# Two interleaved attention layers: the second follows five steps behind the first instead of eight, and the feed-forward runs on 64+64 tokens every two steps

## The chip, the cores and the metric

The kernel runs on one core of one Trainium2 chip. The metric is device microseconds of one execution; the figure of the kernel before is the median of three runs. A profile of one execution, taken by the hardware profiler, stands beside it. Engines are named as in the profile: PE (TensorE matmul), PEld (its weight loads), DVE (VectorE), ACT (ScalarE), POOL (GpSimd), SP (SyncE, which issues most DMAs).

## What is computed

The reference takes 2048 tokens of width 576 and applies attention, feed-forward, attention, feed-forward, each with a layer norm before it and a residual sum after it. Both attention layers use the same weights, both feed-forwards too. Cut to what matters:

```python
def _A_ref(x, mem0, Wq, Wk, Wv, Wo, seg_len):     # 32 heads of 128, 8 memory rows, segments of 32
    mem = mem0
    for s in range(n_seg):                         # 64 segments, one after the other
        xs = x[:, s * seg_len:(s + 1) * seg_len, :]
        h = jnp.concatenate([mem, xs], axis=1)     # 40 rows
        q, k, v = h @ Wq, h @ Wk, h @ Wv           # per head
        p = softmax(where(mask, q @ k.T * scale, -1e9))
        o = (p @ v) @ Wo
        mem = o[:, :M, :]                          # the next segment needs this
        outs.append(o[:, M:, :])
def _B_ref(x, w1, w3, w2):                         # 576 -> 4608 -> 576
    return (silu(x @ w1) * (x @ w3)) @ w2
x = x + _A_ref(_layernorm(x), ...); x = x + _B_ref(_layernorm(x), ...)
x = x + _A_ref(_layernorm(x), ...); x = x + _B_ref(_layernorm(x), ...)
```

The memory rows tie each segment to the one before it, so a layer's 64 segments are a chain.

## The kernel before, in words

**Steps.** The work goes in steps. Step t computes segment t of layer one and segment t − LAG of layer two together, as one operand of 80 columns (twice 32 tokens and 8 memory rows). With LAG = 8 there are 72 steps: 0 to 7 hold layer one alone, 8 to 63 both layers, 64 to 71 layer two alone. A one-layer step has operands of 40 columns.

**A step on PE** consists of batches, each with a letter (`KINDS`): eight Q (queries and keys of four heads, 32 matmuls) with eight q (their last 64 of the 576 rows, as two row tiles side by side), four S (scores of a group of eight heads), four T (transposed probabilities), four P (values), four O (output projection, 32 matmuls) with four o (its last 64 columns, as column tiles). Values: in two-layer steps they are computed for a pair of steps, four G with tails g (`vg`, 128 rows by 512 columns) and one narrow V with tail v (`vm`, memory rows of the even step); one-layer steps use X and V. The results of a G go to the tile V in two halves of 64 rows (`vg_out`), the second after the P of its group.

**Feed-forward.** A job (`job`, L454) takes 128 tokens of each layer, every four steps: p (transposes of the attention output, `post_tr`), two layer norms with transposes n into XTB, then 18 units of 256 hidden columns: F (`ffn_up`, 16 matmuls of 256 columns) with tail f, tanh on ACT, two products on DVE, and for each two units and each layer a W or w (`ffn_down`, 8 matmuls of 288 columns) that DVE adds to the residual XR. There are 18 jobs: the first two and the last two hold one layer only (128 columns). Each job but the last streams all feed-forward weights from HBM through SP: per unit w1, w3 (`load_w13`, four DMAs into one of two W13 slots) and w2 (`load_w2`, one of two W2C slots); a slot is loaded again when the F or W that read it is done. The last job's weights replace the attention weights in the tiles W and WV (`tail_load`). After its job a layer-one group gets a layer norm of its own (L1tr, letter b) and is written into HT, the transposed input of the attention; layer one's own inputs (L0tr, letter a) are loaded through SP and normed in groups of 128.

**Order.** The order of PE is a string of letters, `FIRST + FOUR * 11 + LAST` (16 steps, 11 times four steps, 12 steps and the final job). `plan` (L76) places the work of the other engines, queue by queue, around it by list scheduling with a cost for each node (`actc`, `dve`, `EW_LAT`, `dma_bw`) and slots of limited pools (`POOLS`: PSUM banks, W13, HTT and so on); each engine then runs its instructions in that order and waits on semaphores where it must. PE batches have a tiling mode (full, column, row, or smaller tiles); batches that may run in either full or column mode take the mode of their neighbours, and in column mode `mm` (L586) issues each matmul as two of 64 columns of weights.

**Helpers.** All PE instructions stand at L591, ACT at L594, DVE at L597, SP's DMAs at L600; in the profile they are told apart by tiles. POOL clears the tile PB (L1010) and takes the power in the layer norm (L760).

Of the kernel before, what the change touches and what calls it, by code (L numbers as in the profile page):

```python
# [7 lines left out]
BF = mybir.dt.bfloat16  # L8
# [15 lines left out]
NPR = FF // (2 * P)  # L24
# [4 lines left out]
LAG = 8  # L29
R_HT = 6  # L30
# [3 lines left out]
EW_LAT = 0.135  # L34
NOW = 1.0e18
POOLS = {"bank": 8, "qkt": 4, "sme": 2, "pb": 2, "pts": 1, "ot": 4,
         "xr": 3, "xn": 2, "w13": 2, "w2": 2, "htt": 4}


def role(t):  # L40

    return (t - LAG) % 2
# [9 lines left out]
class Node:  # L52
# [11 lines left out]
    def after(self, *more):  # L64
        for d in more:
# [6 lines left out]
KINDS = {"m0tr": "m", "L0tr": "a", "L1tr": "b", "POST": "p", "Ftr": "n", "QK": "Q", "QKt": "q", "SC": "S", "TR": "T", "PV": "P",  # L72
         "WO": "O", "WOt": "o", "VX": "X", "VXt": "x", "VM": "V", "VMt": "v", "FF": "F", "FFt": "f", "VG": "G", "VGt": "g", "W2": "W", "W2b": "w"}


def plan(nodes, pools, letters):  # L76
# [42 lines left out]
    while len(order) < len(nodes):  # L119
# [46 lines left out]
        for m in n.outs:  # L166
            m.ready = max(m.ready, n.end + (0.0 if m.eng == e == "PE" else n.lat))
            m.left -= 1
            if m.left == 0:
                push(m)  # L170
# [5 lines left out]
def actc(*ns):  # L176

    return sum(max(0.067 + n * 0.000833, 0.19) for n in ns)


def dve(*ns):
    return sum(max(0.065 + n / 960.0, 0.19) for n in ns)


def dveh(*ns):

    return sum(max(0.065 + n / 1920.0, 0.19) for n in ns)
# [6 lines left out]
def ewh(*ns):  # L194
# [3 lines left out]

FIRST = (
    "amQQQQqqqqSSqqQQQTSQqqSxXVvPTPTOPOOTooPoOoQQqqqqQSQvqqSVQQqTqSQPQOSToPXTOPTxoPOOooQqqqQQSVvqQQSQqqqQSqTQPOSTPTOP"  # L200
    "OToooPaOoQQqqqqQQSvSVQqqqQQQSqTPSXTOPTOPoTxoPOOooQQpQqqqvVqSnQQSFfqFQqfqqQTQSPFTfSOFPWOToPFToffPOOooWQqqqqQQSQQS"
    "FFfqfVvqTQWQqSFxffqQFPSXTWfPFTOPOTOPFOooooWQfqqqQQSFqfqVvQQSFfqTQPWQSqqfFTQOSfoPFTOPWFTOPooffOoFQqqQqqvSQQWSVqqf"
    "FQQWqqSTQPQSTOPabOTXPooTOPxxOooXqqpQQQqqSQnVvfSFTQqqqQQPSFffqQFTOPoSWTFfPOOTFPWOooofQQqfqqFSQFqqfgQGWTQPQSfqFQQq"
    "fqFSWTGFSggfGPGTOPOTfgFaPOOooooWVvqqfQQFFQSqfqQWQSqqfFQTQQqfqSFPWTSFPOTfoOPFWTOPffFOoooWQQqqqqQSbQQQqgqSGSTGPQTq"
    "gqQPOggSGTGPOTOPoooOoQqqqpQVpSQnQvqqqQnQFSTffqFQQPqSwTFPSffOOWTFPFTOPWOoooowFffqqQQQWSfqqFQwQSFqfqgGTQQPWfqSTFFg"
    "gfqGQwPGTOoSPFgfOGTOPWOoooFqqfqQQQQvSwqVSFqqfQQWwTFPQfqfqFTQSwPWSfFOTFPWwOTffFPOOaooooWQQqqqqQwSbQGQgqqSQTQPQqqg"
    "SGTSGPGggTOPOTOPoooOo"
)
FOUR = (
    "QvqqpQQpQqqVSSnnQQFqfqfFQTQfqqWSFPwTFPSfOOTFPwTOPWOooooFffqqQQQQqqSWFSFffqgGQTQPQQgqqqGSwTFPGSfgfgFTGOPOWTOPwOoo"  # L210
    "ooFqqQQQQqfqVvSSwWFfqfqQQTFWQwQSFffqqFPWTOPSowTFPffOTOFPWwOoooFqqfqQQQWQSqqqaQSQQbQqgqSGTSGPgTGPOTggOPGTOPwOoooo"
)
LAST = (
    "QqqqpQQQSnpQQqqqVSvTSnQFffqPFOQqTwPoSWTFPffFTOOWPwOoooFFqfqQQQqqfSQQwQfqqFTSGSqfgQFPWQgfqGTSFPGFTfggOOPGTOPwWOoo"
    "ooFFqffqQQwQWQSqqVSvqqQQTFQPSfqqQwTOWSPFTFPofOTOPwOoooWFfqfqQQQQqfqSFwWvVSFTfqqQQPWQqqSvTQVSPOTbOPwOTooPoxOoXqQp"
    "pVvQqqqQSQQnqqSQnqQFTSfqQPFTSOPfTFOPwTOPWOooooFqfqfQQQSVqqqvQQQwSfqFWTFPSfqqQTQOPSFTwfFPOTOPWOooooFfqqQQQSqfxvVX"
    "qfFQwWTSQFQqqqfQPWSTwFPffqQFTWSOwFPffOFTOPwOooooWFvqfqQQQSWqqVQwSFfqqfQFTQQSqqWPQTPSOoTOPwOToobPxOoXqqqQQQpvSVqQ"
    "qQSnqQFfSTQFPqqfQOTSFfPwTOoofPFTOPFOfoowQqqQFSQfqqqQQSVvqqfQFTQFSfqPQOTowPSFTfxXPOTOPFOooowVvqqQQQSqqfQQSqqfQFST"
    "QQPwqqFTSOfPFTOfPwTOPfoooOoFQQqqqqQSQQSqqQVvSfTFPqQQwqfTSFPOTOFPTOPfoooOoFpwnfffFFwFwfffFFFwfffFFwFwfffFFFwfffFF"
    "wFwfffFFFfww"  # L220
)
ORDER = FIRST + FOUR * 11 + LAST


class Opt:

    qk, qkt, sc, tr, pv, wo, wog, vm = 0.0079, -0.0342, 0.0268, 0.1447, 0.0406, 0.2653, 0.0725, 0.1407
    vmt, vx, vxt, ff, fft, win, w2, gstep = -0.0231, 0.2313, 0.0843, 0.2124, -0.1839, 0.8 * (LAG - 4), 0.1943, 0.0624
    ustep, mode_pen, hor, wait, bulk, ff_split, last_win, tail_at = 0.0315, 0.1194, 0.0162, 0.141, 0.02, False, 2.5, -1.5


def make_nodes(em, nseg, pools, o=Opt, dma_bw=230e3, load_bw=400e3):

    ngrp = nseg // 4
# [10 lines left out]
    nst = nseg + LAG  # L245
    kb = lambda rows, cols: rows * cols * 2

    def layers_of(t):
        return [li for li in (0, 1) if 0 <= t - LAG * li < nseg]

    def both(t):

        return len(layers_of(t - role(t))) == 2

# [5 lines left out]
    ld_t = [load("ldt", kb(3 * R64, 4096), -10.0, em.load_tails(0)), node("ACT", 0.1, em.load_tails(1), prio=-120, name="ldt", lat=6.0)]  # L260
    node("ACT", 0.1, em.load_tails(2), prio=-80, name="ldt", lat=6.0)
    ld_h = [load("ldqk", kb(512, 4096), half - 9.0, em.load_qk(half)) for half in (0, 1)]
# [4 lines left out]
    m0t = node("PE", 0.3, em.m0_tr(b[0]), deps=[ld_m0], prio=-5, mode="full", acq=b, name="m0tr")  # L267
    m0e = node("DVE", 0.5, em.m0_ev(b[0]), deps=[m0t], prio=-5, rel=b, name="m0ev")

    xr = {}  # L270
    ht_ready = {}
    reads_ht = {}
    yx = {}
    ht_mem = {t: [] for t in range(nst + 1)}
    steps = [{} for _ in range(nst)]

    def ln_nodes(tag, src, xn, deps, prio, writes, warm=False):

        a = node("DVE", 1.16, em.ln_stats(src, xn), deps=deps, prio=prio, acq=[] if src is xn else [xn], name=tag + "stats")
        p_ = node("POOL", 0.45, em.ln_pow(xn), deps=[a], prio=prio, name=tag + "pow")  # L280
        c = node("DVE", 0.46 if src is xn else 0.66, em.ln_norm(src, xn), deps=[p_], prio=prio, name=tag + "norm")
        b = Slot("bank", users=len(writes))
        d = node("PE", 5 * 0.056, em.ln_tr(xn, b, warm), deps=[c], prio=prio, mode="full/col", acq=[b], rel=[xn], name=tag + "tr")
        out = []
        for wr, cost, more in writes:
            out.append(node("AD", cost, wr(b), deps=[d] + more + out[-1:], prio=prio, rel=[b], name=tag + "wr"))
        return out

    def ht_writes(li, g):

        out, at = [], {}
        for j in range(4):
            at.setdefault((4 * g + j - role(4 * g + j + LAG * li)), []).append(j)
        for te, js in at.items():
            te += LAG * li - R_HT
            cost = ewh(240, 80, 80) if li and both(te + R_HT) else ewh(160 * len(js))
            out.append(((lambda js: lambda b: em.ht_write(li, g, js, b))(js), cost, reads_ht.get(te, []) + reads_ht.get(te + 1, [])))
        return out

    def ht_set(li, g, nodes_):  # L300
        i = -1
        for j in range(4):
            t = 4 * g + j + LAG * li
            i += j == 0 or role(t) == 0
            ht_ready[li, t] = nodes_[i]


    vx_ev, last_v, pvs = {}, [], {}

    def v_nodes(name, t, k, prio, tail_at, emit, strips, deps, tail_deps, free):  # L310

        modes = ("col", "quad") if strips[0][3] == R64 else ("c32", "oct")
        b = banks()
        m_ = node("PE", 8 * 0.2158, emit(b, False), deps=deps, prio=prio, mode=modes[0], acq=b, name=name)
        n = node("PE", 0.2158, emit(b, True), deps=deps + tail_deps, prio=prio + tail_at, mode=modes[1], acq=b, name=name + "t")
        reads_ht.setdefault(t, []).extend([m_, n])
        for r in (0, 1):
            outs = em.v_parts(strips, r)
            b[r].users = len(outs)
            for p0, width, row, blk in outs:  # L320
                e = node("AD", (0.55, 0.6), em.v_ev(b[r], p0, width, row, blk), deps=[m_, n] + free.get(blk // 2, []), prio=prio + 0.01 * (blk // 2),
                         rel=[b[r]], name=name + "e")
                vx_ev.setdefault((name, t, blk // 2), []).append(e)
        return [m_, n]

    def paired(t):

        return role(t) == 1 and both(t) and t + 1 < nst and both(t + 1)

    def vg_nodes(t, g, deps, tail_deps):  # L330

        b = banks()
        for s in b:
            s.users = 2
        m_ = node("PE", 8 * 0.2158, em.vg(t, g, b, False), deps=deps, prio=t + o.vm, mode="full/col", acq=b, name="VG")
        n = node("PE", 0.2158, em.vg(t, g, b, True), deps=deps + tail_deps, prio=t + o.vm, mode="row", acq=b, name="VGt")
        for s in (t, t + 1):
            reads_ht.setdefault(s, []).extend([m_, n])
        return b, [m_, n]

    def vg_out(t, g, b, deps, row):

        return [node("AD", (0.55, 0.6), em.v_ev(b[r], row, R64, row, 2 * g + r), deps=deps, prio=t + o.vm + 0.01 * g + (0.05 if row == 0 else 0.0), rel=[b[r]],
                     name="VGe") for r in (0, 1)]

    def vx_pair(t, prio):

        if t and paired(t - 1):
            return
# [982 lines left out]
```

## Time and profile before

| | us |
|---|---|
| median of three runs (2683.0 to 2690.0) | 2684.11 |
| profiled execution, first to last instruction | 2684.2 |
| PE busy | 2621.2 (98%) |
| DVE busy | 2111.8 (79%) |
| ACT busy | 1346.4 (50%) |
| POOL busy | 332.2 (12%) |
| DMA engines, mean share | SP's queue 38.7%, 120 GB/s in all |
| TensorE clock granted | 0.995 of full |

The span of the profiled execution equals the median of the runs to 0.1 us, so sums made against the profile hold for the runs too. Engine times are sums of what each engine is busy; a busy PE is the union of pipelined matmuls, whose ends are modelled, so the cost of a batch is read from the start of its first matmul to the start of the next batch. In the timeline a row is "start us, duration us, engine, line, operation, tiles, shape, count"; successive instructions of one kind are merged into one row, and a row's duration holds some 0.16 us of pipeline that overlaps the next row. A step's end is read from the copy into the tile YO (ACT), one for each step: the first, of step 0, starts at 58.3 us, that of step 3 at 125.1, of step 7 at 238.2, of step 63 at 2403.6, of step 71 at 2641.6.

### The profile page before, as it was taken

What the parts mean: (1) busy time and instruction counts of PE and PEld (TensorE: products, weight loads), DVE (VectorE), ACT (ScalarE), POOL (GpSimd) and SP (SyncE); (2) the same over time, 40 slices, a digit from 0 to 9 for tenths busy, and PEclk for the clock granted to TensorE, in tenths of its full rate; (3) what the DMA queues carried; (4) which work ended last, traced back from release to release, by engine and by line L of the source; (5) the groups of instructions that cost most, each with busy time, mean ns of one, the idle gap of its engine ahead of it and who ended that gap; (6) DMA issues with size and microseconds to landing.
All of it is one profiled execution on the core that took longest, in us unless ns stands there. A gap on an engine that the chain in (4) does not pass through costs nothing.

```text
span 2684.2 us, 136846 instructions
## 1 busy us (share of the span) xinstructions
PE 2621.2 (98%) x60881; PEld 2292.9 (85%) x60933; DVE 2111.8 (79%) x5485; ACT 1346.4 (50%) x3916; POOL 332.2 (12%) x400
## 2 busy tenths in 40 slices
PE   5999999999999999999999999999999999999998
PEld 4888888889888888988888898888889888888887
DVE  4787887887888778787877878787787878687876
ACT  2655554454545455454544545454454545455453
POOL 1111110110111011011101101110110111011110
PEclk8999999999999999999999999999999999999999
DMA  9064524344342434434333443423344342334457
GB/s 319 4 178 118 166 72 125 97 120 118 99 127 84 114 99 119 118 100 126 88 112 97 120 118 100 126 87 113 98 120 118 102 126 82 114 98 130 125 169 256
DMA packets 478178, 322.08 MB, mean 120 GB/s; under 512 B 26024, under 2 KB 467760, under 8 KB 476944
## 3 DMA queue, kind: packets, MB, share of 16 engines
q1 hardware_dynamic: 474048, 305.43, 38.7%
q8 instruction: 477, 7.82, 1.2%
q0 software_dynamic: 3024, 6.93, 0.9%
q10 hardware_dynamic: 512, 0.94, 0.2%
q14 instruction: 117, 0.96, 0.1%
HBM read 308.49 MB, written 2.36 MB: 116 GB/s over the span
## 4 chain that ended last, share of the span: by engine, by line
PE 89%; DMA 3%; DVE 3%; ACT 3%; issue 1%; SPq 1%; ACTq 0%; DVEq 0%
PE bank L591 89%; ACT V L594 1%; SPq L600 1%; DMA W<-in_B_w_dram 1%; DMA W<-in_A_Wk_dram 1%; DVE STAT L597 1%; DVE SME L597 0%; DMA WO<-in_A_Wo_dram 0%; DVE V L597 0%; DVE HTT L597 0%; DVE PB L597 0%; DMA XN<-in_A_x_dram 0%; ACT SME L594 0%; DVE PTS L597 0%; ACT PTS L594 0%
## 5 line engine op out<-in xcount | busy, mean ns | idle before, releaser
L591 PEld LDWEIGHTS <-W 128*128 128x128 bf16 (+2 forms) x32064 | 1267.3, 100 | 118.8 <-issue 55.7
L591 PE MATMUL bank<-HT,W 128*128 128x80 bf16 (+3 forms) x23040 | 807.0, 197 | 14.9 <-ACT HT L594 5.7
L591 PE MATMUL bank<-XTB,W 128*64 128x256 bf16 (+5 forms) x9024 | 664.3, 263 | 4.6 <-DMA W<-in_B_w_dram 3.1
L594 ACT ACTIVATE QKT<-bank 128x256 bf16<-128x256 f32 (+2 forms) x1477 | 343.2, 314 | 362.1 <-PE bank L591 334.1
L1010 POOL MEMSET PB<- 128x1024 bf16 x288 | 273.9, 951 | 1888.4 <-PE bank L591 1537.4
L591 PE MATMUL bank<-OT,WO 128*128 128x80 bf16 (+3 forms) x11520 | 410.9, 198 | 4.6 <-issue 2.0
L591 PEld LDWEIGHTS <-WO 128*128 128x128 bf16 (+1 forms) x11520 | 381.4, 102 | 30.4 <-issue 17.7
L594 ACT ACTIVATE V<-bank 32x512 bf16<-32x512 f32 (+1 forms) x594 | 335.8, 585 | 110.9 <-PE bank L591 104.5
L591 PE MATMUL bank<-WV,HT 128*32 128x512 bf16 (+4 forms) x3628 | 366.2, 383 | 5.5 <-issue 3.2
L591 PE MATMUL bank<-W2C,HTT 128*64 128x288 bf16 (+1 forms) x3040 | 320.1, 287 | 0.8 <-DMA W2C<-in_B_w_dram 0.4
L597 DVE TENSOR_REDUCE STAT<-SME 104x8 f32<-104x320 f32 (+1 forms) x576 | 274.6, 477 | 18.2 <-ACT SME L594 12.4
L597 DVE TENSOR_TENSOR PB<-SME,STAT 40x128 bf16<-40x128 f32 (+4 forms) x912 | 274.9, 335 | 11.3 <-POOL PB L1010 0.5
L594 ACT ACTIVATE HTT<-bank 128x512 bf16<-128x512 f32 (+1 forms) x324 | 177.6, 557 | 196.8 <-PE bank L591 195.5
L591 PEld LDWEIGHTS <-HT 128*32 128x32 bf16 (+4 forms) x3680 | 158.1, 99 | 120.3 <-issue 17.9
L591 PEld LDWEIGHTS <-HTT 128*64 128x64 bf16 (+1 forms) x3104 | 229.4, 104 | 32.1 <-issue 0.6
L597 DVE CAST QKT<-bank 128x128 bf16<-128x128 f32 (+4 forms) x571 | 154.5, 317 | 123.4 <-PE bank L591 122.4
L597 DVE SCALAR_TENSOR_TENSOR XR<-bank,XR 128x288 f32<-128x288 f32 x576 | 239.6, 446 | 13.8 <-PE bank L591 10.9
L597 DVE SCALAR_TENSOR_TENSOR HTT<-HTT,bank 128x512 bf16<-128x512 bf16 (+1 forms) x324 | 202.1, 624 | 56.1 <-ACT HTT L594 51.8
L594 ACT ACTIVATE OT<-bank 128x320 bf16<-128x320 f32 (+1 forms) x425 | 157.0, 405 | 169.5 <-PE bank L591 165.5
L597 DVE TENSOR_TENSOR HTT<-HTT,bank 128x512 bf16<-128x512 bf16 (+1 forms) x324 | 203.6, 628 | 29.0 <-PE bank L591 1.4
L594 ACT ACTIVATE PTS<-bank 128x320 bf16<-128x320 f32 (+1 forms) x395 | 148.2, 404 | 132.3 <-PE bank L591 95.7
L594 ACT ACTIVATE SME<-SME 104x320 f32<-104x320 f32 (+1 forms) x288 | 135.3, 470 | 153.4 <-DVE SME L597 151.1
(61 smaller groups left out, 1837.7 us busy)
## 6 DMA issues: line engine op xcount, KB each, us to landing
W<-in_B_w_dram SPq DMA_DIRECT2D x612, 256.0 KB, 3.7
W2C<-in_B_w_dram SPq DMA_DIRECT2D x306, 288.0 KB, 3.3
W<-in_B_w_dram SPq DMA_DIRECT2D x612, 32.0 KB, 3.3
W<-in_B_w_dram SPq DMA_DIRECT2D x8, 1024.0 KB, 10.5
W<-in_A_Wq_dram SPq DMA_DIRECT2D x9, 512.0 KB, 9.7
WO<-in_A_Wo_dram SPq DMA_DIRECT2D x4, 1152.0 KB, 17.7
XR<-in_A_x_dram POOLq DMA_DIRECT2D x16, 288.0 KB, 3.4
WV<-in_B_w_dram SPq DMA_DIRECT2D x4, 1152.0 KB, 11.3
```

Of the source, the lines that this page charges most:

```text
L591: self.ch("PE", self.nc.tensor.matmul(out, lhsT=lhsT, rhs=rhs, start=start, stop=stop, skip_group_check=True, **k))
L594: self.ch("ACT", self.nc.scalar.activation(*a, **k))
L597: self.ch("DVE", getattr(self.nc.vector, fn_)(*a, **k))
L600: self.ch("SP", self.nc.sync.dma_start(out=out, in_=in_))
L1010: return lambda n: self.ch("POOL", self.nc.gpsimd.memset(self.T.PB[:, pb.i], 0.0))
```

## The change

LAG goes from 8 to 5, so there are 69 steps: 0 to 4 with layer one alone, 5 to 63 with both, 64 to 68 with layer two alone. Steps are paired by a table (`pairing`) that begins anew at steps 5, 64 and 65. A job now takes 64 tokens of layer one (rows 0 to 63 of the residual tile) and 64 of layer two (rows 64 to 127) every two steps, so 34 jobs; the first three and job 32 hold one layer, the last one 128 tokens of layer two. A job has nine units of 512 hidden columns: F has 32 matmuls of 128 columns, W one batch for both layers. w1 and w3 come as two DMAs of 512 KB into three slots (W1), the last 64 rows of both as two of 64 KB into two slots (WT), w2 as two of 288 KB into three slots (W2C). One layer norm (Ltr, letter b) serves 64 tokens of layer one's input, read from the residual tile, and 64 of layer two's; HT has two slots of step pairs instead of three. The columns within HT, V, QKT and PB are laid out anew: the values of a pair go to V by one copy of 128 rows, QKT of even steps by one copy, PB by two pieces in even steps and four in odd ones. The output rows are written as bfloat16 by DVE (`ffn_fin`) instead of by an ACT copy. POOLS, the planner's costs and all order strings are new, and XN and HTT are cleared by POOL at the start. Core of the diff:

```diff
-NPR = FF // (2 * P)
+NU = FF // (4 * P)
-LAG = 8
-R_HT = 6
+LAG = 5
-EW_LAT = 0.135
+EW_LAT = 0.15
-POOLS = {"bank": 8, "qkt": 4, "sme": 2, "pb": 2, "pts": 1, "ot": 4,
-         "xr": 3, "xn": 2, "w13": 2, "w2": 2, "htt": 4}
+POOLS = {"bank": 8, "qkt": 4, "sme": 2, "pb": 2, "pts": 1, "ot": 3,
+         "xr": 3, "xn": 2, "w1": 3, "wt": 2, "w2": 3, "htt": 2}
+def pairing(nseg):
+    out, at = {}, 0
+    for lo, hi in ((0, LAG), (LAG, nseg), (nseg, nseg + 1), (nseg + 1, nseg + LAG)):
+        for t in range(lo, hi):
+            at += t > 0 and (t - lo) % 2 == 0
+            out[t] = (at, (t - lo) % 2)
+    return out
-            m.ready = max(m.ready, n.end + (0.0 if m.eng == e == "PE" else n.lat))
+            m.ready = max(m.ready, n.end + (0.0 if m.eng == e else n.lat))
 def actc(*ns):
-    return sum(max(0.067 + n * 0.000833, 0.19) for n in ns)
+    return sum(0.051 + n * 0.000833 for n in ns)
 def dve(*ns):
-    return sum(max(0.065 + n / 960.0, 0.19) for n in ns)
+    return sum(max(0.065 + n / 960.0, 0.13) for n in ns)
+PERIOD = (
+    "qqQQQQqfgqFSSWGGgqqfQTQPFTOQQqqgSoWGSPFTGfgPOTOPWOoooFpWqqfQQQQfqqSFSnvVWQTQqfqFSWQPQTfqqFSPWTOPOfoWFobTOPWOooFf"
+)
...
-ORDER = FIRST + FOUR * 11 + LAST
+ORDER = FIRST + PERIOD * 27 + LAST
-def make_nodes(em, nseg, pools, o=Opt, dma_bw=230e3, load_bw=400e3):
+def make_nodes(em, nseg, pools, o=Opt, dma_bw=290e3, load_bw=345e3):
...
     def job(j):
+        last = j == npair + 1
+        s0 = nst if last else 2 * j + 2
+        rs = slice(R64 if j == npair else 0, P if j >= 3 else R64)
...
+        for at, u in enumerate([NU - 1] + list(range(NU - 1)) if last else range(NU)):
...
+                for kind in (0, 1):
+                    ld.append(stream("w1", kb(512, 512) / dma_bw, em.load_w1(u, kind, w1[kind]), prio=prio - 1 + 0.001 * kind, acq=[w1[kind]], name="W1l"))
+                ld.append(stream("wt", kb(128, 512) / dma_bw, em.load_wt(u, wt), prio=prio - 0.997, acq=[wt], name="WTl"))
+                for h in (0, 1):
+                    ld.append(stream("w2", kb(256, 576) / dma_bw, em.load_w2(u, h, w2[h]), prio=prio - 0.99 + 0.001 * h, acq=[w2[h]], name="W2l"))
...
     def ffn_up(...):
-            for fb in range(2):
-                fs = slice(fb * P, (fb + 1) * P)
-                os_ = slice(fb * 2 * P + lo, fb * 2 * P + hi)
+            for fb in range(4):
+                os_ = slice(fb * P + rs.start, fb * P + rs.stop)
...
     def ffn_down(...):
             for half in range(2):
-                for i in range(2):
-                    W = self.tail_w[2 * pp + i][1] if last else self.T.W2C[:, w2s[i].i]
-                    for fb in range(2):
-                        self.mm(self.bk(b[half])[:, 0:288], self.T.HTT[:, htts[i].i, fb, bi * P:(bi + 1) * P],
-                                W[:, fb, half * 288:(half + 1) * 288], i == 0 and fb == 0, i == 1 and fb == 1)
+                for fb in range(4):
+                    self.mm(self.bk(b[half])[:, 0:288], self.T.HTT[:, htt.i, fb, :], w[2](fb, half * 288, (half + 1) * 288), fb == 0, fb == 3)
...
     def p_at(self, t):
         if not self.both(t):
-            return [(0, 0, 24, 8), (0, 8, 64, 32)] if role(t) else [(0, 0, 80, 16), (0, 16, 0, 24)]
-        if role(t):
-            return [(0, 0, 72, 40), (1, 0, 112, 16), (1, 16, 48, 24)]
-        return [(0, 0, 80, 16), (0, 16, 0, 24), (1, 0, 24, 24), (1, 24, 64, 16)]
+            return [(0, 0, QW * self.role(t), QW)]
+        if self.role(t):
+            return [(0, 0, 96, SEG), (0, SEG, 0, MEM), (1, 0, MEM, 24), (1, 24, SW, 16)]
+        return [(0, 0, 0, QW), (1, 0, QW, QW)]
...
-    T.HT = sp.tile([P, R_HT // 2, 5, 2 * SW + 2 * MEM], BF, name="HT")
+    T.HT = sp.tile([P, 2, 5, 2 * SW], BF, name="HT")
-    T.W13 = sp.tile([P, pools["w13"], NCH, 2 * P], BF, name="W13")
+    T.W1 = sp.tile([P, pools["w1"], 4, 4 * P], BF, name="W1")
+    T.WT = sp.tile([P, pools["wt"], 4 * P], BF, name="WT")
     T.W2C = sp.tile([P, pools["w2"], 2, D], BF, name="W2C")
-    T.HTT = sp.tile([P, pools["htt"], 2, 2 * P], BF, name="HTT")
+    T.HTT = sp.tile([P, pools["htt"], 4, P], BF, name="HTT")
+    nc.gpsimd.memset(T.XN[:], 0.0)
+    nc.gpsimd.memset(T.HTT[:], 0.0)
```

## Prediction

> **What bounds the kernel now.** I read the page first: its busy times, then the chain that ended last.
>
> ```profile
> PE 2621.2 (98%) x60881; PEld 2292.9 (85%) x60933; DVE 2111.8 (79%) x5485; ACT 1346.4 (50%) x3916; POOL 332.2 (12%) x400
> PE 89%; DMA 3%; DVE 3%; ACT 3%; issue 1%; SPq 1%; ACTq 0%; DVEq 0%
> ```
>
> PE is busy nearly throughout and is 89% of the chain. As a busy PE may still be waiting, I went to the longest pieces of the chain and to the busy times of one stretch:
>
> ```profile
> 1537.60 71.42 PE bank L591 x1582
> 1693.95 71.42 PE bank L591 x1581
> 1850.30 71.42 PE bank L591 x1581
> ```
>
> ```profile
> 1693.95:1850.30 156.35, 155.55 (x3469) 137.42 (x3473) 125.07 (x324) 79.16 (x229) 18.54 (x22) 1.00 0.38 109
> ```
>
> The same piece returns every 156.35 us, four steps. In one such period PE is busy 155.55, DVE 125.07 (80%), ACT 79.16, the DMA engines 38% at 109 GB/s. So the question is how much PE time each batch takes, from its start to the next row's start. PE's timeline, from several places:
>
> ```profile
> 1695.46 1.31 PE L591 MATMUL bank<-OT,WO 128*128 128x80 bf16 x32
> 1696.60 0.45 PE L591 MATMUL bank<-PTS,V 128*128 128x80 bf16 x8
> 1696.89 1.31 PE L591 MATMUL bank<-OT,WO 128*128 128x80 bf16 x32
> ...
> 1700.86 1.15 PE L591 MATMUL bank<-W2C,HTT 128*128 128x288 bf16 x8
> 1701.84 2.01 PE L591 MATMUL bank<-OT,WO 128*128 128x80 bf16 x64
> ...
> 1251.94 1.92 PE L591 MATMUL bank<-XTB,W 128*128 128x256 bf16 x16
> 1253.69 1.14 PE L591 MATMUL bank<-W2C,HTT 128*128 128x288 bf16 x8
> ...
> 1323.58 1.91 PE L591 MATMUL bank<-XTB,W 128*128 128x256 bf16 x16
> 1325.42 0.32 PE L591 MATMUL bank<-HT,W 64*128 64x80 bf16 x8
> ...
> 313.11 1.95 PE L591 MATMUL bank<-XTB,W 128*128 128x128 bf16 x32
> 314.90 1.27 PE L591 MATMUL bank<-HT,W 128*128 128x80 bf16 x31
> ```
>
> An O takes 1.14 to 1.15 us, a P 0.29, a W 0.98, an F of 16 matmuls of 256 columns 1.75. Where a different tiling follows the same F, it takes 1.84: a switch costs about 0.097. The fifth pair matters most: 32 matmuls of 128 columns (two units of the first jobs in a row), the form that the change makes of every F, take 1.79 us.
>
> **PE's work, part by part.** Counts come from the letters of the two orders (switches: walking through them with each letter's tiling mode), prices from start-to-start distances as above.
>
> | batches | before → after | us each | change, us |
> |---|---|---|---|
> | Q, two-layer / one-layer steps | 448/128 → 472/80 | 1.149 / 0.82 | −11.8 |
> | O, likewise | 224/64 → 236/40 | 1.149 / 0.82 | −5.9 |
> | q, o, S, T, P, likewise | 1568/448 → 1652/280 | 0.137, 0.146, 0.26, 0.287, 0.287 / 0.10, 0.11, 0.21, 0.205, 0.205 | −7.3 |
> | G, X with tails | 118 → 132 | 1.946 | +27.2 |
> | V with tail | 46 → 33 | 1.87 | −24.3 |
> | F, f: 256 columns of both layers | 252 → 0 | 1.964 | −494.9 |
> | F, f: 256 columns of one layer | 72 → 0 | 1.021 | −73.5 |
> | F, f: 512 columns, 128 tokens | 0 → 270 | 2.015 | +544.1 |
> | F, f: 512 columns, 64 tokens | 0 → 36 | 1.07 | +38.5 |
> | W, w | 288 → 306 | 0.98 | +17.6 |
> | transposes | 97 → 102 | 0.28 | +1.4 |
> | switches | 1090 → 1032 | 0.097 | −5.6 |
>
> Before sums to 2569.2 us, after to 2574.7: **PE's work grows by 5.5 us**. Three steps fewer save some 25, and the finer feed-forward gives it back: a unit of 512 columns at 128 tokens costs 0.05 more than one of 256 at 256, and 36 W of one-layer jobs run half empty. The one form without a row is the 64-column matmul: between the 40-column one (0.82 for 32) and the 80-column one (1.149), so the 36 units are worth −4 to +7 us beside the 0.95 that I take for their F.
>
> The Trainium skill speaks against this: TensorE: Matmul & The Clock Gate, section Back-to-back issue gap, gives about 81 ns for each matmul of 128 columns in a sustained stream of weight loads and matmuls. The rows at 313.11 and 314.90 have 1.79/32 = 56 ns. By the page's figure 270 units of 32 would cost 216 us more, an estimate, and the kernel would be far slower; the measurement decides.
>
> **PE's waiting.** The span less 2569.2 is 115.0 us. Held against the step ends (YO rows) it lies here: 38.9 in step 0, 24.0 in steps 1 to 7, 27.0 in the 56 two-layer steps (0.48 each), 14.6 in steps 64 to 71 (12.1 in the last five), 10.5 after the last step.
> - Step 0 ends at 58.3, after the last loads of WO; the same loads stay: 38.9. New there: POOL clears XN before the first load of x, which ACT's queue issues. By POOL's memsets (HT 2.30 us for 2640 elements, YTS 1.15 for 1280, both now smaller) that ends near 6 us, and the load at 1.37 moves there. Behind it in that queue are the loads of mem0 and of half of WV's tail. The transposes at 13.27 come up to 4.5 later, but the first QK at 23.96 follows waits for Wk at 17.6 and 21.5, which hide it; without that cover, 4.5 us.
> - Steps 1 to 4 at the 3.4 of steps 1 to 7: 13.7. The last five 12.1, the end 10.5, as now.
> - Two-layer steps: unknown, as each wait depends on the new order. Below: near nothing, 0.1 a step. Above: 0.9, what the worst of today's take. I take 0.40, near today's 0.48, because one wait visibly goes. PE's row below waits for HT after the last o of a step (from that o to the first Q 0.54 us instead of 0.04); in PERIOD an F, 1.79 us, stands behind both last o's.
>
> ```profile
> 1781.00 1.31 PE L591 MATMUL bank<-HT,W 128*128 128x80 bf16 x32 [0.34 <-ACT HT L594]
> ```
>
> 59 × 0.40 = 23.6. Sum of the waiting: 38.9 + 13.7 + 23.6 + 12.1 + 10.5 = 98.8. **2574.7 + 98.8 = 2673.5, I say 2673**, 11 us (0.4%) under the profiled 2684.2, and so under the median. Each 0.1 us of waiting in every two-layer step is 5.9 us.
>
> **Off PE**, costed at nothing while PE hides it:
> - Copies of values: a G gave four copies of 64x512, now two of 128x512. Today 32x512 and 64x512 take the same (583 and 587 ns on ACT, 686 and 685 on DVE), so 128 rows should too: 8 copies, some 5 us, less in two steps (none less if time went with rows). QKT of even steps saves 16 times about 0.2, PB and YTS a little. DVE and ACT get room, worth nothing unless a PE wait hung on them.
> - Layer norms, transposes back, tanh, products, residual adds: per four steps as many as before, of the same free size. POOL issues 64-token loads and stores twice as often, and it idles most of the span. HT, OT and HTT have fewer slots; in the new order each is reread a batch or more before its next write, so 0, at most the 0.3 a step that sits in my upper end.
> - Weights: 33 jobs instead of 17 stream them: 15.9 MB in some 78 us, 204 GB/s where 102 was needed. While busy, SP's queue moved 305.43 MB in 38.7% of 2684 us, 294 GB/s: enough on average, with 69% busy, and early on the trace shows 381 GB/s.
>
> ```profile
> W<-in_B_w_dram SPq DMA_DIRECT2D x612, 256.0 KB, 3.7
> W2C<-in_B_w_dram SPq DMA_DIRECT2D x306, 288.0 KB, 3.3
> ```
>
> **Rivals.**
> 1. *The weight stream arrives late (slower).* Three W1 and three W2C slots hold one and a half units, so the second half of a unit can load only after the F or W before it. In PERIOD W follows W after T O P O f o (3.5 us), ooo F p and others (3.8) and F o b T O P (4.1); F follows F at the nearest after 4.7 and 4.8. Against this, a W2C load lands in 3.3 us (2.7 to 5.4), and a 512 KB one, 256 KB more at 294 GB/s, in about 3.7 + 0.9 = 4.6. For it: all five distances lie within 1 us of that, and SP's queue is in order. If W2C takes 4.0 and W1 4.9, PE loses 0.7 + 0.3 = 1.0 us in two steps, 27 us over 27 periods: 2700. It decides from 0.4 us a period (11 us) on. DMA engines near 57% or more and "DMA" as releaser of PE would show it.
> 2. *More waits go than I take off.* DVE and ACT work about 9% less (18 of 204 us in four steps), every step's end has a cover: 0.12 a step instead of 0.40: 2657.
> 3. *It does not do what it says: no gain.* The three steps saved are those with the least PE work, and the ramp must carry a whole weight stream for 64 tokens in two steps of some 26 us, 15.9 MB or 300 GB/s, at what the queue delivers. Then steps 2 to 4 wait 2 us more each, and the two-layer steps keep 0.48: 2673 + 6 + 5 = 2684.
> 4. *DVE's order becomes the limit.* It is at 80% now; S to T needs seven DVE and ACT instructions in a row, and the shortest stretch between an S and its T is 5.2 us in both orders, by the letters' prices. A step waiting 0.9: 2673 + 59 × 0.5 = 2703.
>
> **How the numbers follow.** My forecast (2664 to 2681, waits of 0.25 to 0.53 a step) has a chance of 0.35, rival 2 0.20, rival 3 0.20, rival 1 0.15, rival 4 0.10. The range, 2656 to 2706, runs from 0.1 to 0.95 us of waiting a step and so takes in the two unknowns. About 0.3%, 8 us, is what a measurement of this kernel can tell from no change. Faster by over that is under 2676: all of rival 2 and most of the forecast, 0.20 + 0.30 = 0.50. Within it: rival 3 and the rest of the forecast, 0.25. Slower, over 2692: rivals 1 and 4, 0.25.
>
> **What would show it.** Right: a repeating PE piece of 78 to 78.7 us (two steps); F of 32 matmuls 1.79 us apart; steps 1 to 4 hold 96 us of PE work by the same prices, so YO of step 4 near 168; the last YO some 41 us before the end; DMA near 200 GB/s; V copies of 128x512 at 0.59 and 0.69. Wrong: a period over 79.3 us with DMA named before PE's F or W (rival 1), or DVE and ACT before T and P (rival 4); F at 2 us or more (the price of 128 columns); YO of step 4 after 175 (rival 3).

## The result, and the profile after

The changed kernel takes 2870.0 us (median of 4 runs, 2867.6 to 2880.4) against 2686.3 for the kernel before on the same chip: a ratio of 1.069, 95% interval 1.0668 to 1.0712. It is slower by 184 us; the forecast was 2673. The profiled execution took 2880.4, the slowest of the four, with a span of 2878.6. All times here are medians of executions at a granted clock of 0.96 or more, which in e10 below are three of four.

First the page of the changed kernel, parts 1, 3 and 4: busy times, DMA queues (packets, MB, share of the span of 16 DMA engines), the shares of the chain that ended last.

```profile
PE 2685.4 (93%) x71722; PEld 2396.1 (83%) x71725; DVE 2010.8 (70%) x4883; ACT 1237.9 (43%) x3401; POOL 338.9 (12%) x424
...
q1 hardware_dynamic: 539296, 558.04, 63.4%
q8 instruction: 561, 9.19, 1.3%
...
PE 85%; issue 6%; DMA 5%; DVE 3%; ACT 1%; SPq 0%; POOL 0%; DVEq 0%; ACTq 0%; POOLq 0%
```

The two queue lines of the kernel before, which the prediction did not show:

```profile
q1 hardware_dynamic: 474048, 305.43, 38.7%
q8 instruction: 477, 7.82, 1.2%
```

PE is idle 193 us instead of 63, although DVE and ACT do less. The weights (q1) now keep the DMA engines busy 63% of the time. The chain names "DMA" for 5%, which rival 1 expects, but "issue" for 6%: time for which no row gives a cause. To see those pieces I read the chain over two periods, 1200 to 1360 us (start, length, what; x counts matmuls):

```profile
1219.84 34.97 PE bank L587 x982
1254.81 0.73 issue
...
1302.13 13.48 PE bank L587 x387
1315.61 2.26 issue
1317.87 20.12 PE bank L587 x497
1337.99 1.52 issue
1339.52 5.00 PE bank L587 x128
1344.52 1.21 issue
1345.73 8.64 PE bank L587 x256
1354.37 1.31 issue
1355.68 4.33 PE bank L587 x120
```

Before, the longest pieces were 71 us and came back every 156; here they break off again and again, and several whole ones hold 128 or 256 matmuls. As each matmul has its weight load, 128 matmuls are 256 PE instructions. PE's timeline at two of the breaks (start, length, engine, operation, idle time before it in brackets):

```profile
1354.17 0.20 PE L587 MATMUL bank<-HT,W 64*128 64x80 bf16 x2
1355.68 2.50 PE L587 MATMUL bank<-HT,W 64*128 64x80 bf16 x69 [1.31 <-issue]
```

```profile
1425.59 1.14 PE L587 MATMUL bank<-OT,WO 128*128 128x80 bf16 x27
1427.22 0.35 PE L587 MATMUL bank<-OT,WO 128*128 128x80 bf16 x5 [0.50 <-issue]
```

PE stops after 2 matmuls of a q, and after 27 of the 32 matmuls of an O. Every operand of an O is there when it begins, so it can wait for no data in its middle. What else it needs are its own instructions. They come on queue q8: 143,665 PE instructions in the trace over 561 packets are 256.1 a packet, 122,047 over 477 before are 255.9, and a packet is 16 KB. The DMA view of three stretches ahead of the break at 1354.4 (the queue lines alone; the shares are of the 16 engines' time in the stretch, which can come out a little over 100%), 1350.5 to 1352, 1352 to 1353.2, 1353.2 to 1354.4:

```profile
q1 hardware_dynamic: 478, 0.48, 102.3%
```

```profile
q1 hardware_dynamic: 362, 0.37, 92.7%
```

```profile
q1 hardware_dynamic: 219, 0.22, 73.2%
q8 instruction: 1, 0.02, 5.3%
```

For 2.7 us weights fill the engines (102 and 93% of their time) and no instruction packet moves; it comes as the stream thins out, takes about a microsecond (median 1.08), and PE goes on 1.3 us after its end. A gap is counted here from the start of one matmul to the start of the next, less the time that its columns take (36 ns for 80, 56 for 128). In the whole trace, 160 gaps of PE over 140 ns end 1.2 to 1.65 us after the end of such a packet, 162 us in all; before there are 40, 22 us. (In other windows of 0.45 us within 4 us of a packet there are 7 to 16 gaps, so a dozen are chance.) I call these gaps **stops**.

Two counts from the trace show that PE is out of instructions at a stop. Number PE's instructions from the first on, in blocks of 256: 147 of the 160 stops come when 190 to 192 instructions of a block have begun, while a gap that has nothing to do with the fetch would fall anywhere in the block. And the packets start late. Take the number of PE instructions begun when a packet starts, less 256 for each packet before it: the median is 279, against 217 in e1 below, which has the same instructions and less traffic. At 20 ns an instruction that is 1.2 us later. For 138 packets it is 320 or more (10 in e1), and a stop follows 119 of these.

The view of waits gives the same quickly in one line, PE waiting for "issue" (us, times, longest), before and after:

```profile
PE bank L591 <- issue: 11.9, 30, 1.6
```

```profile
PE bank L587 <- issue: 130.1, 128, 2.9
...
PE bank L587 <- DMA W2C<-in_B_w_dram: 6.5, 10, 1.3
...
PE bank L587 <- DMA W<-in_B_w_dram: 5.8, 11, 1.0
```

Weights that land late, rival 1, cost PE 12 us. Loads do land later (last column, us from issue to landing; before 3.7 and 3.3, the first for half the size), but mostly still in time:

```profile
W<-in_B_w_dram SPq DMA_DIRECT2D x594, 512.0 KB, 5.0
W2C<-in_B_w_dram SPq DMA_DIRECT2D x594, 288.0 KB, 4.2
```

The forecast's own signs: a period of two steps takes 84.2 us on average (forecast 78 to 78.7); YO of step 4 starts at 183.7 (168); 41 us follow the last YO (41); 32 matmuls of 128 columns are 56 ns apart (1.79/32 = 56); a V copy takes ACT 587 ns (0.59).

### The profile page after: what moved, and what is told of

Same layout as the page of the kernel before. It is cut to its first block, busy times and chain, and to the rows that moved or that the text cites. A ratio compares the mean times of both kernels' runs of the same rounds, so it can differ in the third digit from the quotient of the medians.

```text
span 2878.6 us, 157132 instructions
## 1 busy us (share of the span) xinstructions
PE 2685.4 (93%) x71722; PEld 2396.1 (83%) x71725; DVE 2010.8 (70%) x4883; ACT 1237.9 (43%) x3401; POOL 338.9 (12%) x424
## 3 DMA queue, kind: packets, MB, share of 16 engines
q1 hardware_dynamic: 539296, 558.04, 63.4%
## 4 chain that ended last, share of the span: by engine, by line
PE 85%; issue 6%; DMA 5%; DVE 3%; ACT 1%; SPq 0%; POOL 0%; DVEq 0%; ACTq 0%; POOLq 0%
PE bank L587 85%; DMA W<-in_B_w_dram 2%; DMA W2C<-in_B_w_dram 2%; DVE HTT L593 1%; DMA W<-in_A_Wk_dram 1%; DVE STAT L593 1%; DVE PTS L593 0%; DVE SME L593 0%; ACT OT L590 0%; DVE PB L593 0%; DMA WT<-in_B_w_dram 0%; DVE XR L593 0%; ACT V L590 0%; ACT HTT L590 0%; DVE XN L593 0%
## 5 line engine op out<-in xcount | busy, mean ns | idle before, releaser
L587 PE MATMUL bank<-XTB,W 128*64 128x128 bf16 (+3 forms) x17728 | 592.6, 218 | 56.5 <-issue 49.3
L590 ACT ACTIVATE QKT<-bank 128x256 bf16<-128x256 f32 (+3 forms) x1181 | 318.8, 346 | 388.6 <-PE bank L587 381.0
L587 PE MATMUL bank<-WV,HT 128*64 128x512 bf16 (+4 forms) x3694 | 381.4, 388 | 3.3 <-issue 2.9
L587 PE MATMUL bank<-W2C,HTT 128*64 128x288 bf16 (+1 forms) x3832 | 357.3, 289 | 14.2 <-issue 7.1
L590 ACT ACTIVATE V<-bank 128x512 bf16<-128x512 f32 (+2 forms) x465 | 254.8, 587 | 154.5 <-PE bank L587 152.2
L593 DVE CAST QKT<-bank 128x320 bf16<-128x320 f32 (+3 forms) x387 | 142.0, 398 | 238.0 <-PE bank L587 232.4
L587 PEld LDWEIGHTS <-HT 128*64 128x64 bf16 (+4 forms) x3696 | 208.5, 105 | 97.3 <-issue 30.4
L593 DVE TENSOR_TENSOR PB<-SME,STAT 40x320 bf16<-40x320 f32 (+1 forms) x744 | 265.0, 380 | 24.5 <-DVE STAT L593 0.5
L593 DVE SCALAR_TENSOR_TENSOR XR<-bank,XR 128x288 f32<-128x288 f32 (+1 forms) x608 | 256.9, 450 | 20.0 <-PE bank L587 11.3
L593 DVE SCALAR_TENSOR_TENSOR HTT<-HTT,bank 128x512 bf16<-128x512 bf16 (+1 forms) x306 | 198.5, 649 | 69.8 <-ACT HTT L590 67.6
L593 DVE TENSOR_TENSOR SME<-bank,maskb 104x320 f32<-104x320 f32 (+1 forms) x276 | 134.1, 486 | 124.5 <-PE bank L587 116.8
```

The lines of the kernel that those rows point to most:

```text
L587: self.ch("PE", self.nc.tensor.matmul(out, lhsT=lhsT, rhs=rhs, start=start, stop=stop, skip_group_check=True, **k))
L590: self.ch("ACT", self.nc.scalar.activation(*a, **k))
L593: self.ch("DVE", getattr(self.nc.vector, fn_)(*a, **k))
```

## The experiments

My theory, A: the weight stream holds up PE's instruction packets, and PE stops. Rivals: B, the weights themselves are late; C, PE has too many instructions, whatever the DMAs do. Stops, counted as above, and PE's waits by the view of waits:

| kernel | us | ratio to before, 95% | stops, us | PE for issue | PE for W + W2C | q1 busy |
|---|---|---|---|---|---|---|
| before | 2686 | 1 | 22 | 11.9 | 4 | 38.7% |
| changed | 2870 | 1.0668 to 1.0712 | 162 | 130.1 | 12 | 63.4% |
| e1 less traffic | 2720 | 1.0107 to 1.0137 | 19 | 12.0 | 0 | 30.4% |
| e2 F unsplit | 2799 | 1.0391 to 1.0442 | 54 | 41.5 | 15 | 65.7% |
| e3 before, more traffic | 2733 | 1.0150 to 1.0187 | 41 | 29.8 | 13 | 57.4% |
| e4 short rows | 2804 | 1.0427 to 1.0472 | 98 | 68.1 | 6 | 69.8% |
| e5 half loads | 2799 | 1.0401 to 1.0453 | 96 | 66.4 | 6 | 64.9% |
| e6 all short | 2864 | 1.0652 to 1.0681 | 85 | 37.6 | 90 | 69.6% |
| e7 long rows of w2 | 2876 | 1.0685 to 1.0724 | 149 | 119.4 | 17 | 62.6% |
| e8 halves, F unsplit | 2764 | 1.0286 to 1.0321 | 32 | 24.3 | 12 | 66.2% |
| e9 before, short rows | 2689 | 1.0002 to 1.0022 | 11 | 7.9 | 9 | 40.2% |
| e10 64-byte transfers | 2982 | 1.1087 to 1.1151 | 231 | 193.3 | 26 | 70.1% |
| e11 two of them | 3179 | 1.1819 to 1.1862 | 286 | 235.9 | 122 | 73.5% |
| e12 uneven cut | 2990 | 1.1070 to 1.1188 | 212 | 171.7 | 49 | 71.9% |
| e13 SP idle 0.5 us | 2843 | 1.0572 to 1.0603 | 128 | 101.0 | 10 | 64.2% |
| e14 SP idle 1.5 us | 2812 | 1.0450 to 1.0513 | 82 | 65.1 | 22 | 66.6% |
| e15 quarter loads | 2818 | 1.0484 to 1.0519 | 41 | 23.2 | 62 | 65.8% |

### What the stops are: e1, e2, e3

e1 in load_w1 (load_w2 likewise, one of two blocks), e2 in ffn_up around the four matmuls of a block, e3 in the kernel before, behind each unit's loads of w1 and w3:

```diff
+            m = 4 if self.full1 <= 3 else 1
+            self.dma(self.T.W1[:, s.i, 0:m], src[:, 0:m])
```

```diff
+                        was, self.mode = self.mode, "full"
                         for c in range(4):
...
+                        self.mode = was
```

```diff
+            self.dma(self.T.more[self.more % 4], (self.a.w1, self.a.w3)[pr % 2][0:4 * P, fb:fb + 512])
```

> The changed kernel with smaller weight transfers: from the fourth load of each kind on, a load of w1 or w3 brings 128 of its 512 rows and a load of w2 half of its 256, so the feed-forward computes with stale rows. As many DMAs, waits and PE instructions as in the changed kernel; about 6 MB in two steps instead of 15.7, less than the kernel before has in that time (8). Theory A (PE's instructions come in packets of 16 KB, 256 instructions each, which wait behind the weight packets, and PE stops where one comes late; 162 us of stops that end 1.2 to 1.65 us after such a packet in the changed kernel, 22 before): the stops fall to about the 22 of before and the waits for W and W2C (14 us) go: 2700 to 2735 us. Theory B (the weights themselves land late, rival 1 of the prediction): 2680 to 2740 as well, but then with the stops that no landing ends unchanged in share. Theory C (the number of PE instructions alone is too high, whatever the DMAs do): 2850 to 2870, nothing but the 14 us of landings goes.

> The changed kernel with F never split into two 64-column tiles: 15,744 weight loads and matmuls fewer (127,708 against 143,452; the kernel before has 121,868), the same transfers and waits, and 422 more switches of tiling, which cost 422 x 0.097 = 41 us of PE. Theory A: instruction packets are needed 11% more rarely, but the weight packets still delay them: half of the 162 us of stops goes, 41 come: 2790 to 2860. Theory B: no landing becomes earlier, so 2870 + 41 = 2890 to 2915. Theory C: the stops fall to about before's, as the number of instructions nearly does: 2870 - 140 + 41 = 2755 to 2785.

> The kernel before, with one more transfer of 512 KB from w1 or w3 into scratch memory ahead of every unit of 256 columns: 160 MB more in all, some 170 GB/s instead of 109 (the changed kernel has 200). Nobody reads the copies and no slot is held by them; PE's instructions are the same. Theory A: instruction packets are delayed as well, though they are needed more rarely than in the changed kernel: stops with the cause 'issue' appear in the middle of PE's batches, 2715 to 2790. Theory B: the weights land later behind the extra transfers, so waits named W and W2C appear, but none named 'issue': 2690 to 2720. Theory C: unchanged, 2680 to 2690.

All three fall where A puts them: 2720, 2799, 2733. With less traffic the same 143,452 weight loads and matmuls run nearly without stops, so C is out; with the same traffic and 11% fewer instructions two thirds of the stops go, so lateness of the weights (B) is not it, and the 2799 carries some 35 us of added switches (360 more by the trace, at 0.098; the 422 that I had reckoned with were too many). With 57% instead of 39% of the engines' time taken, the kernel before gets stops, too, and loses 45 us. The busiest group of F, in the changed kernel and in e1 (busy, mean ns of one | idle before it), shows what goes and what stays:

```profile
L587 PE MATMUL bank<-XTB,W 128*64 128x128 bf16 x14592 | 464.3, 220 | 46.3 <-issue 41.1 <-DMA W<-in_B_w_dram 3.8 <-DMA WT<-in_B_w_dram 1.2
```

```profile
L587 PE MATMUL bank<-XTB,W 128*64 128x128 bf16 x14592 | 451.0, 220 | 0.0
```

e1 has no stops left to speak of, and its chain is regular: the same pieces return after 79.8 us, with a wait for DVE between them.

```profile
1213.53 17.35 PE bank L587 x420
...
1233.10 23.51 PE bank L587 x654
...
1293.36 17.35 PE bank L587 x420
...
1312.92 23.51 PE bank L587 x654
```

Yet e1 is 1.2% slower than the kernel before. So even with instructions and weights in time the change would have lost some 33 us; that part is taken up below.

### What sets the delay: e4 to e7, and e9

First idea, A1: an instruction packet waits behind a number of weight packets, so their length counts. Against it A2: the size of the DMA counts.

e4 and e5 in load_w1, e6 like e4 and besides in load_w2 (load_wt likewise), e7 in load_w2; e9 is the kernel before with load_w2 as in e6, and in tail_load w1 and w3 in four pieces of 256 columns, w2 in two halves of its rows:

```diff
+            for h in (0, 256):
+                c0 = u * 512 + h
+                self.dma(self.T.W1[:, s.i, :, h:h + 256], (self.a.w1, self.a.w3)[kind][0:4 * P, c0:c0 + 256].rearrange("(c p) f -> p c f", p=P))
```

```diff
+            for c in (0, 2):
+                self.dma(self.T.W1[:, s.i, c:c + 2], src[:, c:c + 2])
```

```diff
+            for d0 in (0, D // 2):
+                self.dma(self.T.W2C[:, s.i, :, d0:d0 + D // 2], self.a.w2[fa:fa + 2 * P, d0:d0 + D // 2].rearrange("(b p) d -> p b d", p=P))
```

```diff
-        return lambda n: self.dma(self.T.W2C[:, s.i], self.a.w2[fa:fa + 2 * P, :].rearrange("(b p) d -> p b d", p=P))
+        return lambda n: self.dma(self.T.W2C[:, s.i], self.a.w2[fa:fa + 2 * P, :].rearrange("(p b) d -> p b d", p=P))
```

> The changed kernel with each 512 KB load of w1 or w3 as two DMAs of 256 columns each, in rows of 512 bytes (those of the kernel before) instead of 1024: same bytes, twice as many packets of w1 and w3, 594 more DMAs. It asks whether the length of a row sets how long an instruction packet waits. Theory A with the wait counted in packets of the others (one turn each): shorter turns, some of the 162 us of stops goes, 2790 to 2850. Theory A with the wait counted in bytes or in busy time of the DMA engines: no gain, and with more packets the engines are busier: 2870 to 2930. Theory B: the loads take longer, 2880 to 2930, with W named in front of PE. Theory C: 2865 to 2880.

> The changed kernel with each 512 KB load of w1 or w3 as two DMAs of 256 rows each: as many DMAs and bytes as in the kernel with short rows, but the packets stay 1024 bytes long (46 ns each by the trace, 27 for 512 bytes). Theory A1 (an instruction packet waits its turn behind a number of weight packets already handed to its DMA engine, so the time of one packet counts): unchanged, 2855 to 2885, with about 160 us of stops. Theory A2 (smaller DMAs let the instruction packet in sooner, whatever their rows): near the short rows' 2804, 2790 to 2830.

> The kernel with short rows, with the loads of w2 and of the tails of w1 and w3 cut in the same way: no weight packet of the feed-forward over 576 bytes (w2's were 1152, 51 ns). A1: of the 98 us of stops that the short rows of w1 and w3 left, half goes: 2745 to 2785. A2: as many bytes and more packets, so no better than the 2804, 2800 to 2840.

> The changed kernel with two neighbouring rows of w2 in each partition, so that its packets are 2304 bytes (some 100 ns) instead of 1152, and half as many; the rows of w2 then meet the wrong columns of w1 and w3 and the feed-forward computes something else, with the same work. A1: the instruction packets wait longer, stops of 190 to 240 us in place of 162: 2900 to 2950. A2: the DMA engines have fewer packets and are less busy, so unchanged or less: 2840 to 2872.

> The kernel before, with w2's rows cut to 576 bytes and the last loads of w1, w3 and w2 cut to 512 and 576 bytes. Its 22 us of stops lie in the first 270 us (11 us) and in the last 200 (7 us). A1: the part behind weight packets of 1152 and 2048 bytes goes, 5 to 12 us: 2673 to 2682, the only candidate so far to beat both kernels. A2: unchanged, 2683 to 2692.

A1 falls on e5 and e7: halves with the long rows gain as much as the short rows did, and rows of 2304 bytes change nothing (2876 within the changed kernel's runs). In e6 the stops fell a little further, but SP, which needs about 0.5 us to issue a DMA, now issues 12 in a unit instead of 6, and the weights are late: the lost time only changes its name.

```profile
PE bank L587 <- DMA W2C<-in_B_w_dram: 56.0, 56, 2.9
PE bank L587 <- issue: 37.6, 53, 3.1
PE bank L587 <- DMA W<-in_B_w_dram: 33.5, 42, 1.9
```

In e9 nothing is won: 11 us of stops go, and the time is that of before or 3 us more. PE waits for W 8.0 us instead of 3.1 and for W2C 1.4 instead of 0.4, which accounts for half of the 11; the other half I have not traced. My expectation had counted only the stops.

### Two trials that changed the DMA engines instead: e10, e11, e12

Halving a load does two things, and A2 can be read either way: it halves the DMA that an engine is at, which an instruction packet might have to wait out (A2a), and it lets SP issue the same bytes more slowly, so that less stands ahead of an instruction packet (A2b).

e10, behind each load of w1 or w3 (e11 twice), and e12 in load_w1:

```diff
+                self.dma(self.T.more[self.more % 8], self.a.w1[0:1, 0:32])
```

```diff
+            for p0, p1 in ((0, 112), (112, P)):
+                self.dma(self.T.W1[p0:p1, s.i], src[p0:p1])
```

> The changed kernel with its 512 KB loads of w1 and w3 whole, but one transfer of 64 bytes into scratch memory issued behind each, which nobody reads; SP takes about 0.51 us to issue any DMA by the trace, so the next load follows 0.5 us later, as it does between two halves. In the kernel with loads halved by rows the stops fell from 162 to 96 us although the packets stayed as long, so A1 is out. Theory A2a (the instruction packet waits until the DMA whose packets its engine is at has ended, 32 x 46 ns = 1.5 us of a 512 KB load, 0.75 of a half): whole loads, so unchanged, 2855 to 2885. Theory A2b (the instruction packet waits behind all that SP has issued up to then; the more slowly SP issues, the less that is): as with halves, 2790 to 2825, with stops of 80 to 115 us.

> The same with two such transfers behind each load of w1 or w3, 1.5 us from one load to the next, which is what 512 KB take the 16 DMA engines. A2a: unchanged, 2855 to 2885. A2b: little piles up any more, stops of 40 to 80 us; but the weights start later, and each wait for W and W2C counts: 2760 to 2815.

> The changed kernel with each load of w1 or w3 cut at partition 112 into two DMAs of 448 and 64 KB: as many issues of SP as with halves, the same bytes in the same packets of 1024 bytes, no transfer added. The pacing with 64-byte transfers did not settle between A2a and A2b, as these transfers themselves held the DMA engines (busy 70.1% of 2980 us instead of 63.4% of 2879, some 264 us more). A2a (the instruction packet waits until the DMA that its engine is at has ended): the large part still takes 28 x 46 ns = 1.3 us of an engine instead of 1.5, so only a little goes, 2840 to 2870, stops of 135 to 160 us. A2b (it waits behind all that SP has issued, and slower issuing leaves less): as with halves, 2790 to 2820, stops of 85 to 110 us.

All three became slower than either theory allows, and decide nothing between them. Their weights are the same packets, but these took the engines longer: the time of all packets of 1024 and 1152 bytes together, per engine, rose from 1745 us to 2000, 2233 and 2059. In e10 and e11 a few packets were held up for long (99 of 100 w2 packets took under 376 ns in the changed kernel, under 689 and 1132 here); in e12 the usual packet of 1024 bytes took 53 ns instead of 46. For A they are further cases in which busier engines go with more stops; the busy share alone does not set them, as e4 has 98 us of stops at 69.8% and e10 231 at 70.1%.

### Slower issuing without a transfer: e13, e14; quarters: e15

e13, behind each load of w1 or w3 (e14 with 27 instead of 9), and e15 in load_w1:

```diff
+            for _ in range(9):
+                self.ch("SP", self.nc.sync.drain(fusable=False))
```

```diff
+            for c in range(4):
+                self.dma(self.T.W1[:, s.i, c], src[:, c])
```

> The changed kernel with whole loads of 512 KB, and 9 drain instructions on SP behind each load of w1 or w3, of 58 ns from one to the next by the trace: 0.5 us in which SP issues nothing and no byte more is moved. A2a (an instruction packet waits until the DMA that its engine is at has ended): unchanged, 2850 to 2885. A2b (it waits behind all that SP has issued; slower issuing leaves less): as with halves, 2785 to 2825.

> The same with 27 drains, 1.5 us, so that the next load is issued when the one before it is nearly through. A2a: unchanged but for later weights, 2855 to 2900. A2b: stops down to 40 to 70 us, waits for W and W2C perhaps 20 to 40 us more: 2760 to 2820.

> Each load of w1 or w3 as four DMAs of 128 KB, rows of 1024 bytes: an engine is 0.37 us at one of them, and w2's loads of 0.8 us are now the longest. SP needs 12 issues or some 6.2 us in a unit of 8.9. A2a: stops of 55 to 80 us, 2755 to 2800. A2b: the same stops if no more than the slower issuing counts; the run does not part the two, but tells how much the remedy is worth at its best, and whether the weights become late (waits for W and W2C over 30 us, then 2800 to 2860).

Idle time of SP alone, at the same DMAs, takes 27 us off (0.5 us) and 58 us (1.5 us); A2a foresaw no change. So A2a alone is out: at the same DMAs, a slower issue is a faster kernel, as A2b says. That an instruction packet stands behind what SP has issued is A2b's reading of it, as no view shows the queue; the trace shows that fewer packets start late (320 or more in the count above: 113 and 87 instead of 138). But 0.5 us gave 27, not the 71 of the halves, which issue at the same pace; the shorter DMA, or that only half of a load is out at first, must count as well. Which of the two stays open. The quarters bring the stops down to 41 us and lose more by late weights than e5:

```profile
PE bank L587 <- DMA W2C<-in_B_w_dram: 52.2, 52, 3.1
PE bank L587 <- issue: 23.2, 32, 3.1
```

### Both remedies: e8

e5's loads with e2's F.

> Two remedies together: loads of w1 and w3 in halves of 256 rows (2799 alone) and F never split (2799 alone, 41 us of it added switches). If the same stops are cured twice, about 22 to 35 us of stops stay: the 54 of F unsplit less 20 to 30 us, 2765 to 2785. If the halves take as much off as they did alone (66 us): 2735, more than the stops that are left.

2764, a microsecond below the overlapping case: 32 us of stops are left. It is the fastest version of the changed order that computes everything, and still 3% behind the kernel before. No version here beats the kernel before.

## Why the prediction was wrong, point by point

**The step that failed is the one on the weights** under "Off PE": "294 GB/s: enough on average, with 69% busy". I priced the doubled stream only by when weights land, and PE's instructions only as PE time. The bytes are enough on average (PE waits 12 us for them), but PE's instructions travel on the same engines: stops rose by 140 us. The line for it stood in the page of before, 477 packets in q8, as did PE's waits for "issue" in the middle of work; I read neither. The Trainium skill states the rule: Runtime: NRT & Kernel Launch, section Instruction fetch mechanics, has each engine fetch its next block of 16 KiB, 256 instructions, through a DMA queue of its own while it executes the present one, and calls the cost mostly hidden. Packets of 16 KB for 256 instructions are what the traces show; hidden holds for the kernel before (22 us of 2684) and not for this one (162 of 2879).

**What came out larger.** The span is 205 us over the sum (2878.6 to 2673.5). Between e1 and the changed kernel lie 163: 143 of stops, 13 of waits for weights, and some 10 in which PE works on at half the granted clock, less a few us of e1's own waits that go. The clock was 0.5 for 70 us here and for 32 in e1; the five stretches at 0.5 between 330 and 1920 us, of 3.4 us each, begin within 4 us of the start of a stop of over 2 us. The other 42 are in e1 as well, and are three sizes:
- PE's work in a period: 78.6 us, summed from e1's trace, against 77.8 by my prices, both with 28 switches at 0.097 to 0.098. A third of a microsecond lies in the S (0.30 us each instead of 0.26: two of the eight pause twice for some 0.1 us, at matmuls that wait for a copy to QKT), the rest is about 0.1 each in q, F with its tail, G, V and T. Over 27 periods this is 23 us. Against the kernel before it is less: summed in the same way, its four steps hold 155.4 us of work where my prices give 154.5, and 0.9 of waits, so half of the 0.48 a step that I called waiting was work that the prices had missed. Held against that, the work of two steps grew by 0.4 us, 11 us over the periods beside the 5.5 of the table, which by itself takes up the 11 us of the forecast gain.
- Waits in a period without stops: 1.19 us (two of 0.49 for DVE, HTT and PTS, and one of 0.20) against my 2 x 0.40: 10.5 us.
- The remaining 8 to 9 us lie outside the periods.

One row of my table has its counts wrong: q, o, S, T and P are 24 batches a step, 1344/384 before and 1416/240 after, not 28; its −7.3 was worked out with 24, so the sum stands.

**What was right.** The prices of F (1.79 for 32), of Q and O (36 ns a matmul), of V's copies. The 56 ns a matmul of F's 128 columns hold in every run here, against the 81 of the page that the prediction weighed. The end of 41 us. Steps 1 to 4: YO of step 4 at 169.0 in e1 against 168; that it came at 183.7 in the changed kernel is stops again, not the ramp of rival 3.

**The rivals.** Rival 1 has the right sign and place, a weight stream that fills the DMA engines (63.4% where it named 57%), a period over 79.3 with DMA in the chain; its victim and size are wrong: 27 us for late weights, while they cost 12 and the late instructions 140. Rivals 2 and 3 fall with the period. Rival 4, DVE's order, is in the 10 us of waits, 0.6 us a step where it said 0.9; but the two longer ones are for HTT and PTS, not between S and T, where it put them. The range ended at 2706; none of my cases had a price above 27 us for the stream, as I had bounded it by landings alone.

## What to carry to other kernels

Count PE's instructions as DMA traffic with a deadline: one 16 KB packet for every 256 (a matmul split into two tiles counts double), and when a change raises both the stream's share of the DMA engines and PE's instructions, look for PE waiting for "issue" in the middle of a batch. Here, with loads of up to 512 KB, stops were small with the engines 30 to 39% busy, visible at 57%, and 5% of the time at 63%; with smaller loads, slower issuing or fewer PE instructions they were 1 to 4% at 65 to 70%. A probe such as e3, more traffic that nobody waits for in the old kernel, gives a first idea in one run of how much room is left. Smaller loads, slower issuing and unsplit matmuls each took back a part, until SP's issuing made the weights themselves late.

## What the runs showed of the hardware that I had not expected

- PE runs out of instructions in the middle of a batch when weights fill the DMA engines: 147 of 160 stops come at one place in the blocks of 256 instructions, and PE goes on 1.2 to 1.65 us after a packet of 16 KB has landed.
- Idle instructions on SP made the kernel faster: 1.5 us behind each load, 594 times, 58 us less.
- 594 transfers of 64 bytes within the chip's memory cost 112 us, 1188 of them 309; one in a hundred w2 packets then took over 689 and 1132 ns, against 376 without them.
- With the loads cut at partition 112 the usual packet of 1024 bytes took 53 ns, with whole loads 46.
